# Layer 0's second product in seven block products on 1 core, and layer 1's activation kept in PSUM

## The chip, the cores and the metric

The kernel runs on 1 core of one Trainium2 chip. The metric is the device time of one execution in microseconds (us); the median of 3 runs of the kernel before is 573.87 us (573.56 to 574.56). Times below are in us, from the span's start, unless marked otherwise.

## The reference

A block-sparse attention feeds two feed-forward layers. Attention: batch 2, 8 heads, 768 positions, head size 64; each query sees its neighbours within 16 positions and one summary for each block of 32 (largest K, mean V), in one softmax. Its output is x, 1536 tokens by 512.

```python
h = x @ w_in                  # layer 0: 512 -> 2048
g = s * (r * r) + b           # r = max(h, 0)
x = g @ w_out                 # 2048 -> 512
h = x @ w_in2                 # layer 1
out = maximum(0.01 * h, h) @ w_out2
```

Inputs and weights arrive as 64-bit floats.

## The kernel before

**Products.** TensorE multiplies numbers of a reduced form of 32 bits, so every operand is split into a high part (a cast) and a low part (the operand less its high part), and one product of a 128x128 weight tile with a 128x512 token tile is three matmuls: high by high, low by high, high by low. ScalarE (ACT) makes the casts, VectorE (DVE) or GpSimd (POOL) the low parts (`split_hi` L426, `split_lo` L432 for weights, `ffn_hi` L467, `ffn_lo` L474 for activations). "A matmul" below is one of these 128x512 matmuls.

**Tiles.** The tokens are three chunks of 512 (c is 0, 1, 2 in the code; chunks 1, 2 and 3 in the text), the 2048 features 16 groups of 128 (`fc`). Groups 0 to 7 are the lower features; groups 8 to 15 are the upper ones, and two of them make a pair j (4 to 7). PSUM has 4 banks of output sums (`acc`), 2 called `h`, and 1 each called `at0` and `at1`.

**Seven block products.** A product whose rows, columns and inner dimension can each be halved is done with 7 products of blocks instead of 8, from sums and differences of blocks of weights (s1 to s4) and of tokens or activations (t1 to t4). The names are `a11, s2, a12, s3, a22, s1, s4`. The two halves of the tokens are chunks 2 and 3. A product's result is added on to others in PSUM or in SBUF.

**Order.** No scheduler orders the engines: each one's instructions are issued in the order in which the Python is written. `HEAD` (L49) is a list of operations written by hand that weaves attention with layer 0 for chunk 1 and for the lower features of chunk 2. After it the program goes on in stages:

1. `quads(0, 4, 0)` (L721): the upper features of chunks 2 and 3. The first product goes through seven block products (`block` L647, `after_block` L672). Activation (`add_act` L662: ScalarE relu, VectorE product) leaves its results in SBUF (`late_g` L614). The second product of chunk 2 is plain: `queue` holds its outputs, and `emit_out` (L711) issues one or two, three matmuls each, after every block.
2. The loop `for k in range(NS)`: the lower features of chunk 3, 8 steps of `first_in`, `chain` (L1173: relu, square, cast, low part) and four `ffn_out` (L483).
3. The loop `for fc in range(NS + 1, NFC)`: the plain second product of chunk 3's upper features (`late_split` L733).
4. Layer 1, chunk 1: 16 steps of the same kind. Here `convert` (L1164) turns loaded weights into 32-bit numbers (`rescale` L392 on ScalarE, `low_bits` L397 on VectorE or GpSimd, `shift` L410 on VectorE), `token_forms` (L589) makes the token forms of layer 1, and `split_x` (L610) splits them.
5. Layer 1, chunks 2 and 3 (`second_layer_end` L1015): both products in seven block products. In the "weave" (`weave_block` L788, `weave_after` L873) a pair's seven products of the first kind run between two blocks of the second kind (`out_unit` L844) of the pair before. The rest of the second product, five of its seven blocks, follows as "late units" (`late_unit` L969), whose operands `late_operands` (L957) splits some units ahead.

Queues: SP issues all loads of weights, `load_next` (L1160) one for each half of a group that has been converted.

## Time and profile before

| | |
|---|---|
| median of 3 runs | 573.87 us (573.56 to 574.56) |
| the profiled execution | 573.7 us |
| its span | 571.9 us |
| busy: TensorE 558.4 us (98%), VectorE 435.3 (76%), ScalarE 371.6 (65%), GpSimd 221.4 (39%) | |
| matmuls of TensorE, all forms | 3123 |
| granted clock of TensorE | full in all 40 slices |
| DMA | 53.38 MB, 93 GB/s |

The profiled execution lies 0.17 us below the median, and its own time is 1.8 us more than its span. A timeline row joins neighbouring instructions of one kind: its start, then its busy time; since TensorE's matmuls overlap in the pipeline, the time that a row takes from its engine is the next row's start less its own. "Idle before" names who ended a wait.

### The profile page before, as it was taken

The numbers are of one execution on the slowest core, as the hardware profiler recorded it, in microseconds if no ns is written. First come the engines' busy times: TensorE is split into PE (matmuls) and PEld (weight loads), VectorE is DVE, ScalarE is ACT, GpSimd is POOL, SyncE is SP. The second block draws the span as 40 slices with busy tenths as digits, with TensorE's granted clock in tenths as the row PEclk, the third lists the DMA queues.
The fourth block names the chain that finished last, engine by engine and source line by source line (L and its number), as shares of the span: only waits on it lengthen the run. The fifth ranks groups of instructions, "written<-read, shape, count | busy, mean of one in ns | idle before, by whom it ended". The sixth has DMA issues, their size and how long they took to land.

```text
span 571.9 us, 9002 instructions
## 1 busy us (share of the span) xinstructions
PE 558.4 (98%) x3123; PEld 445.9 (78%) x3124; DVE 435.3 (76%) x890; ACT 371.6 (65%) x856; POOL 221.4 (39%) x258
## 2 busy tenths in 40 slices
PE   3999999999999999999999999999999999999997
PEld 3567778787778888888888888888888888876885
DVE  5888987765689866666575879999458887889982
ACT  4788858776774655445565666766477677768860
POOL 4344644533254455522542435556234433300000
PEclk9999999999999999999999999999999999999999
DMA  8967766571300000000132524542010000000103
GB/s 322 405 206 257 245 225 205 171 244 54 129 2 1 1 0 2 1 1 1 54 95 82 176 91 136 179 140 82 18 56 0 2 1 1 0 2 1 38 0 110
DMA packets 16581, 53.38 MB, mean 93 GB/s; under 512 B 2041, under 2 KB 2937, under 8 KB 15897
## 3 DMA queue, kind: packets, MB, share of 16 engines
q1 hardware_dynamic: 16104, 52.56, 27.3%
q8 instruction: 24, 0.39, 0.3%
q10 hardware_dynamic: 432, 0.26, 0.1%
q14 instruction: 21, 0.16, 0.1%
HBM read 49.08 MB, written 3.15 MB: 91 GB/s over the span
## 4 chain that ended last, share of the span: by engine, by line
PE 93%; DMA 3%; ACT 1%; DVE 1%; SPq 0%; issue 0%; ACTq 0%
PE acc L493 31%; PE h L444 23%; PE at L793 7%; PE h L793 5%; PE acc L850 4%; PE at L974 3%; PE h L654 3%; PE at L654 3%; PE h L974 3%; DMA vt<-in_v 2%; PE acc L974 2%; PE at L336 2%; PE at L256 2%; PE at L355 2%; PE h L355 1%; PE at L210 1%
## 5 line engine op out<-in xcount | busy, mean ns | idle before, releaser
L493 PE MATMUL acc<-g,wout 128*128 128x512 f32 x756 | 188.2, 392 | 0.0
L493 PEld LDWEIGHTS acc<-g,wout 128*128 128x128 f32 x756 | 140.5, 188 | 30.1 <-issue 0.8
L444 PE MATMUL h<-xt,win 128*128 128x512 f32 x564 | 138.5, 392 | 0.0
L444 PEld LDWEIGHTS h<-xt,win 128*128 128x128 f32 x564 | 104.8, 188 | 22.6 <-issue 1.1
L435 POOL TENSOR_TENSOR win<-w,win 128x512 fp32r<-128x512 f32 x36 | 52.0, 1444 | 51.3 <-ACT win L429 37.8
L415 DVE SCALAR_TENSOR_TENSOR w<-st,w 128x512 int32<-128x512 int32 x64 | 59.1, 928 | 7.3 <-issue 3.2
L429 ACT CAST wout<-w 128x512 fp32r<-128x512 f32 x63 | 39.0, 618 | 26.4 <-PE acc L493 23.1
L435 DVE TENSOR_TENSOR wout<-w,wout 128x512 fp32r<-128x512 f32 x50 | 42.0, 839 | 14.5 <-ACT wout L429 14.1
L395 ACT ACTIVATE st<-st 128x512 f32<-128x512 f32 x64 | 41.1, 671 | 0.9 <-DVE w L415 0.9
L429 ACT CAST win<-w 128x512 fp32r<-128x512 f32 x48 | 29.6, 616 | 13.4 <-PE h L444 7.4
L793 PE MATMUL at<-xt,win 128*128 128x512 f32 x144 | 35.9, 392 | 0.0
L477 DVE SCALAR_TENSOR_TENSOR g<-h,own,g 128x512 fp32r<-128x512 f32 x31 | 23.2, 748 | 12.9 <-ACT g L470 12.9
L793 PEld LDWEIGHTS at<-xt,win 128*128 128x128 f32 x144 | 27.0, 188 | 6.2
L408 POOL TENSOR_SCALAR w<-st 128x512 int32<-128x512 uint8 x30 | 23.2, 772 | 17.8 <-DMA st<-in_w 13.0
L470 ACT ACTIVATE g<-h,own 128x512 fp32r<-128x512 f32 x31 | 21.3, 686 | 10.7 <-DVE h L465 7.3
L405 DVE TENSOR_SCALAR w<-st 128x512 int32<-128x512 int32 x34 | 27.5, 810 | 0.0
L455 ACT ACTIVATE r<-h 128x512 f32<-128x512 f32 x31 | 18.3, 593 | 14.1 <-PE h L444 14.1
L850 PE MATMUL acc<-g,wout 128*128 128x512 f32 x96 | 27.2, 393 | 0.0
L299 ACT ACTIVATE sm<-sm,nm 128x120 f32<-128x120 f32 x64 | 24.4, 387 | 3.5 <-DVE nm L281 3.5
L769 POOL TENSOR_TENSOR win<-q,win 128x256 fp32r<-128x256 f32 x8 | 7.7, 958 | 49.0 <-DVE w L822 28.5
L435 POOL TENSOR_TENSOR wout<-w,wout 128x512 fp32r<-128x512 f32 x13 | 17.7, 1361 | 23.1 <-ACT wout L429 18.2
L457 ACT ACTIVATE r<-h 128x512 f32<-128x512 f32 x16 | 9.6, 598 | 23.3 <-PE h L444 23.3
(308 smaller groups left out, 1101.4 us busy)
## 6 DMA issues: line engine op xcount, KB each, us to landing
st<-in_w SPq DMA_DIRECT2D x64, 512.0 KB, 3.5
vt<-in_v SPq DMA_DIRECT2D x5, 1024.0 KB
kt<-in_k SPq DMA_DIRECT2D x8, 500.0 KB, 5.4
q<-in_q SPq DMA_DIRECT2D x8, 256.0 KB, 3.9
w<-in_vn SPq DMA_DIRECT2D x3, 512.0 KB, 10.2
out<-kt SPq DMA_DIRECT2D x6, 256.0 KB, 2.2
w<-in_q SPq DMA_DIRECT2D x4, 256.0 KB, 12.5
w<-in_v SPq DMA_DIRECT2D x2, 512.0 KB
```

The lines of the kernel that those rows point to most:

```text
L299: nc.scalar.activation(out=sm[:, u, :], in_=sm[:, u, :], func=AF.Exp, bias=nm[:, u : u + 1], scale=-1.0, accum_out=rec[:, u, :],)
L395: nc.scalar.activation(out=high, in_=high, func=AF.Prelu, scale=2.0**-112, alpha=2.0**32)
L405: engine.tensor_scalar(f, low, 29, None, op0=ALU.logical_shift_right)
L415: nc.vector.scalar_tensor_tensor(out=f, in0=high, scalar=3, in1=f, op0=ALU.logical_shift_left, op1=ALU.bitwise_or)
L429: nc.scalar.copy(t[:, 0, :], wf[layer, fc][:, half, :])
L435: engine.tensor_sub(t[:, 1, :], wf[layer, fc][:, half, :], t[:, 0, :])
L444: nc.tensor.matmul(hs[i], lhsT=w[:, a, cc * P : (cc + 1) * P], rhs=xt[c][:, b, cc, :], start=(cc == 0 and a == b == 0), stop=(cc == NCC - ...
L493: nc.tensor.matmul(acc[m], lhsT=w[:, a, ms], rhs=g[:, b, :], start=first, stop=last)
L654: nc.tensor.matmul(banks[j, name], lhsT=t[:, a, cc * P : (cc + 1) * P], rhs=x[b][cc], start=(cc == a == b == 0), stop=(cc == b == 1),)
L793: nc.tensor.matmul(ps, lhsT=t[:, a, cc * P : (cc + 1) * P], rhs=x[b][cc], start=(name in ("a11", "s1") and cc == a == b == 0), stop=(cc == ...
L850: nc.tensor.matmul(po[k, m], lhsT=w[:, a, at : at + P], rhs=g[:, b, :], start=(j == 0 and a == b == 0), stop=(j == NQ - 1 and b == 1),)
L974: nc.tensor.matmul(ps, lhsT=w[:, a, m * P : (m + 1) * P], rhs=g[:, b, :], start=(name in ("s1", "s4") and q == a == b == 0), stop=(q == NQ ...
```

## The change

Layer 0's second product for the upper features of chunks 2 and 3 now takes seven block products too. Stage 1 becomes a weave as in layer 1: a class `Woven` holds it, `z0` for layer 0 (pairs 4 to 7) and `z1` for layer 1 (pairs 0 to 7). Two of the seven blocks (four `out_unit` of a pair) run between the first products; the other five are 20 late units after the lower features of chunk 3, in place of stage 3. Layer 0's part adds to sums that the plain lower features have begun (`part1`, `kept`). A count of 128x512 matmuls in the two programs gives 2,192 before and 2,168 after: the plain outputs were 2 x 8 x 4 outputs of 3 matmuls, 192; now there are 7 x 4 x 2 of 3, 168 (48 woven in, 120 late). The activation stays in PSUM: layer 1's leaky relu runs in place on `hs`, its cast and low part read PSUM; the woven products do relu and square there; the lower features of chunk 3 do the square on ScalarE (`square`), not VectorE. Moved besides: `H47 lp47` (a weight's split) earlier in `HEAD`; `ta6 th6 tlv6` (a token form) into the weave; the low part of `split_x` from GpSimd to VectorE, its work later; of the conversions of layer 1's weights 8 are in layer 0 (11 before) and 24 in layer 1 (21 before).

Matmuls change from 2716 to 2692 instructions on TensorE. All instructions of VectorE go from 892 to 960, ScalarE's from 765 to 831, GpSimd's from 263 to 227.

```diff
-A22 d0 O87 as22 G22 E0 lv45 th4 E1 O85 d0 Y22 ta5 E2 A23 tlv3 as23 g22 O90 th5 ta7 tlv2 tlv5 th7 H47 lp47 tlv4 G23 g23
-ta6 tlv7 th6 O88 tlv6 O91 O89
+A22 d0 O87 as22 G22 E0 lv45 th4 E1 O85 d0 Y22 ta5 H47 lp47 E2 A23 tlv3 as23 g22 O90 th5 ta7 tlv2 tlv5 th7 tlv4 G23 g23 tlv7 O88 O91 O89
...
+    def square(x):
+        nc.scalar.activation(out=x, in_=x, func=AF.Relu)
+        nc.scalar.activation(out=x, in_=x, func=AF.Square)
     def ffn_relu(i):
-        rs[i] = gpool.tile([P, 512], F32, name="r")
         if steps[i][0] == 0:
+            rs[i] = gpool.tile([P, 512], F32, name="r")
             nc.scalar.activation(out=rs[i], in_=hs[i], func=AF.Relu)
         else:
-            nc.scalar.activation(out=rs[i], in_=hs.pop(i), func=AF.Prelu, scale=1.0, alpha=0.01)
+            nc.scalar.activation(out=hs[i], in_=hs[i], func=AF.Prelu, scale=1.0, alpha=0.01)
...
-            nc.scalar.copy(gs[i][:, 0, :], rs[i])
...
-            nc.vector.tensor_sub(g[:, 1, :], rs.pop(i), g[:, 0, :])
+            nc.vector.tensor_sub(g[:, 1, :], hs.pop(i), g[:, 0, :])
...
+        end = NFC - 1 if layer or c == 0 else NS - 1
         for a, b in ((0, 0), (1, 0), (0, 1)):
             first = fc == 0 and a == 0 and b == 0
-            last = fc == NFC - 1 and b == 1
+            last = fc == end and b == 1 and not (layer == 0 and c and m < 2)
...
-        nc.gpsimd.tensor_sub(t[1][at], src, t[0][at])
+        nc.vector.tensor_sub(t[1][at], src, t[0][at])
...
+    WEAVE = (("a11", 0), ("a22", 1), ("s2", 0), ("a12", 0), ("s4", 1), ("s3", 0), ("s1", 0))
+    WITH = {"s2": "t2", "s1": "11", "s3": "12", "a22": "21", "s4": "22"}
+    BANK = {"s4": "w", "s2": "u", "s3": "u", "a22": "u", "s1": "v"}
...
+        def raw_act(self, j, k):
+            ps = self.banks[j, "pu"[k]]
+            if self.layer:
+                self.activate(ps)
+            else:
+                home = self.raw[j, f"{k + 1}1"]
+                nc.scalar.activation(out=home, in_=ps, func=AF.Relu)
+                nc.vector.tensor_mul(ps, home, ps)
+        def raw_hi(self, j, k):
+            ps = self.banks[j, "pu"[k]]
+            t = self.go[j, k] = gpool.tile([P, 2, 512], F32R, name="g")
+            (nc.scalar.copy if self.layer else self.shifted)(t[:, 0, :], ps)
+            nc.scalar.copy(self.raw[j, f"{k + 1}1"], ps)
+        def raw_lo(self, j, k):
+            t, ps = self.go[j, k], self.banks[j, "pu"[k]]
+            if self.layer:
+                nc.vector.tensor_sub(t[:, 1, :], ps, t[:, 0, :])
+            else:
+                nc.vector.scalar_tensor_tensor(
+                    out=t[:, 1, :], in0=ps, scalar=shift_b, in1=t[:, 0, :], op0=ALU.add, op1=ALU.subtract
+                )
...
+        def after(self, j, name):
+            add, head = nc.vector.tensor_add, j == self.first
+            p, u, v = (self.banks.get((j, i)) for i in "puv")
+            if name == "a11":
+                nc.scalar.copy(u, p)
+                if not head:
+                    self.activate(self.raw[j - 1, "22"])
+                    self.out_unit(j - 1, 0, 0)
+                if j > self.first + 1 and self.layer:
+                    self.raw_forms(j - 2, 3)
+                    self.out_forms(j - 2, 0)
...
+            elif name == "a12":
+                self.raw_act(j, 0)
+                if self.layer:
+                    self.raw_hi(j, 0)
+                if not head:
+                    self.raw_lo(j - 1, 1)
+                else:
+                    self.out_lo(j, 0)
+                if head and not self.layer:
+                    self.raw_hi(j, 0)
+                    self.raw_lo(j, 0)
+            elif name == "s4":
+                g12 = self.raw[j, "12"]
+                add(g12, rs.pop((self.layer, j)), v)
+                if j < self.last:
+                    if not self.layer:
+                        self.raw_hi(j + 1, 0)
+                    self.activate(g12)
+                    self.raw_lo(j + 1, 0)
+                    if j + 1 < self.last:
...
+            else:
+                g22 = self.raw[j, "22"]
+                add(g22, g22, v)
+                self.out_lo(j, 1)
+                if not head:
+                    self.raw_forms(j - 1, 1)
+                    self.raw_forms(j - 1, 2)
+                    self.out_unit(j - 1, 1, 1)
...
     def chain(i):
-        ffn_relu(i)
-        ffn_act(i)
+        if steps[i][0]:
+            ffn_relu(i)
+        else:
+            square(hs[i])
         ffn_hi(i)
         ffn_lo(i)
...
-    c1, c2 = NFC, 2 * NFC
-    queue = [("out", c1 + NS - 1, m) for m in range(4)]
-    load_next(3)
-    quads(0, NS // 2, 0)
+    c1, c2, nq = NFC, 2 * NFC, n_ffn1 + NFC
+    z0.homes()
+    part1 = [spare[:, 4 + 2 * m : 6 + 2 * m, :].rearrange("p a n -> p (a n)") for m in range(2)]
+    count = len(z0.order)
+    for n in range(count):
+        z0.multiply(n)
+        if n == 0:
+            z0.out_hi(z0.first, 0)
+            for m in (2, 3):
+                ffn_out(c1 + NS - 1, m)
+                nc.scalar.copy(part1[m - 2], accs[0, 1][m])
+        if n == 1:
+            first_forms(6, nc.vector.tensor_sub, nc.vector.tensor_add)
+            first_hi(6)
+            first_lo(6, nc.vector)
+        if n in (3, 4):
+            ffn_out(c1 + NS - 1, n - 3)
+        if n == 4:
+            z0.po.update({(1, m): accs[0, 1][m] for m in range(2)})
+        if n == count - 3:
+            second_in(c2, 0)
+    z0.raw_lo(z0.last, 1)
+    second_in(c2 + 1, 0, nc.gpsimd)
...
+    for m in range(2):
+        z0.kept["x", m] = gpool.tile([P, 512], F32, name="r")
+        nc.scalar.copy(z0.kept["x", m], z0.po[0, m])
     first_in(c2)
+    second_in(c2, 1)
     chain(c2)
-    emit_out(len(queue))
-    for m in range(4):
+    for m in range(2):
+        z0.out_unit(z0.last, 1, m)
+        ps = z0.po[1, m]
+        nc.vector.tensor_add(ps, z0.kept["x", m], ps)
         x_hi(1, m)
+    load_next(4)
+    last, kept, po, ahead_of = z0.last, z0.kept, z0.po, 4
+    work = [(z0.raw_forms, last, part) for part in (0, 2, 1)]
+    for j in range(z0.first, NQ):
+        work += [(z0.out_forms, j, 0), (z0.out_forms, j, 1)]
...
+            po["u", 0], po["u", 1] = (ps_at.pool.tile([P, 512], F32, name=f"at{m}") for m in range(2))
+            for m in range(2):
+                nc.scalar.copy(po["u", m], kept["x", m])
+        for f, j, part in work[2 * k : 2 * k + 2]:
+            f(j, part)
+        for n in {5: (0,), 6: (1,), 7: (2, 3)}.get(k, ()):
+            z0.operands(n)
+        convert((0, 2, 2, 2, 2, 0, 0, 0)[k], nc.gpsimd)
...
-    for fc in range(NS + 1, NFC):
...
+    acc = accs[0, 2]
+    po["w", 0], po["w", 1] = acc[0], acc[1]
+    for n, (name, q) in enumerate(z0.units):
+        z0.operands(n + ahead_of)
+        if name == "s4":
+            z0.raw_forms(q, 3)
+        if (name, q) == ("s1", z0.first):
+            po["v", 0], po["v", 1] = (ps_h.tile([P, 512], F32, name="h") for _ in range(2))
+        for m in range(2):
+            z0.unit(n, m)
+            if q == last and name in ("s2", "s3"):
+                kept[name, m] = soft.tile((name, m))
+                nc.scalar.copy(kept[name, m], po["u", m])
+                if name == "s3":
+                    nc.vector.tensor_add(po["u", m], part1[m], po["u", m])
+            if q == last and name == "s1":
+                for x, ps in ((kept["s2", m], acc[m]), (kept["s3", m], acc[2 + m])):
+                    nc.vector.tensor_add(x, x, po["v", m])
+                    nc.vector.tensor_add(ps, x, ps)
+    for m in range(2):
+        accs[0, 1][2 + m] = po["u", m]
+        for name in ("s2", "s3"):
+            soft.free((name, m))
+    first_in(n_ffn1)
+    second_in(n_ffn1 + 1, 0, nc.gpsimd)
     for m in range(4):
         x_hi(2, m)
+    chain(n_ffn1)
+    for m in range(2):
+        x_hi(1, 2 + m)
...
-        at -= 1
+        if at < 2:
+            for m in (2 * at, 2 * at + 1):
+                split_x([[xt[1][:, a, c, :] for c in range(4)] for a in range(2)], m, xf[1][m])
+        at -= 2
         if 0 <= at < 10:
             token_forms(at // 5, at % 5)
```

**TensorE, the first round of stage 1.** Before, from the last plain output of HEAD on (L654 is a block of the first product, L493 a plain output; the second word is the PSUM bank that is written):

```order
L493 MATMUL acc_2022<-g_2437,wout_2433 128x512 x3
L654 MATMUL at0_2540<-vt_2295,win_2401 128x512 x6
L654 MATMUL h_2553<-xt2_100,win_2402 128x512 x6
L493 MATMUL acc_2044<-g_2527,wout_2530 128x512 x3
L493 MATMUL acc_1980<-g_2527,wout_2530 128x512 x3
L654 MATMUL at1_2571<-xt1_99,win_2402 128x512 x6
L493 MATMUL acc_2009<-g_2527,wout_2530 128x512 x3
L654 MATMUL h_2591<-vt_2296,win_2401 128x512 x6
L493 MATMUL acc_2022<-g_2527,wout_2530 128x512 x3
L654 MATMUL at0_2604<-xt1_99,win_2401 128x512 x6
L493 MATMUL acc_2044<-g_2582,wout_2585 128x512 x3
```

After (L698 is a block of the first product, L777 a block of the second, L497 a plain output):

```order
L497 MATMUL acc_2044<-g_2439,wout_2417 128x512 x3
L698 MATMUL at0_2537<-xt1_99,win_2403 128x512 x6
L777 MATMUL acc_2550<-g_2502,wout_2465 128x512 x3
L698 MATMUL h_2455<-sm0_2318,win_2404 128x512 x2
L698 MATMUL h_2455<-sm3_2434,win_2404 128x512
L698 MATMUL h_2455<-sm1_2487,win_2404 128x512 x2
L698 MATMUL h_2455<-sm2_2489,win_2404 128x512
L777 MATMUL acc_2567<-g_2502,wout_2465 128x512 x3
L698 MATMUL h_2538<-st_2297,win_2404 128x512 x2
L698 MATMUL h_2538<-st_2298,win_2404 128x512
L698 MATMUL h_2538<-st_2297,win_2404 128x512 x2
L698 MATMUL h_2538<-st_2298,win_2404 128x512
```

The three plain outputs that came one after each block are gone; after the first block comes the first block of the second product, for pair 4.

**VectorE, in that round.** Before (L477 low part of an activation, L435 of a weight, L668 and L695 additions out of PSUM, L670 the product that makes the square):

```order
L477 SCALAR_TENSOR_TENSOR g_2527<-r_2471,own_94,g_2527 128x512
L435 TENSOR_TENSOR wout_2530<-w_1043,wout_2530 128x512
L695 TENSOR_TENSOR w_1043<-w_1043,at0_2540 128x512
L668 TENSOR_TENSOR at0_2540<-w_959,at0_2540 128x512
L670 TENSOR_TENSOR w_959<-w_959,at0_2540 128x512
L668 TENSOR_TENSOR h_2553<-w_1043,h_2553 128x512
L670 TENSOR_TENSOR w_1043<-w_1043,h_2553 128x512
L477 SCALAR_TENSOR_TENSOR g_2582<-r_2523,own_94,g_2582 128x512
```

After (L671 and L735 low parts of weights, L753 the square's product in PSUM, L766 the low part of the activation, L842 the addition of s4):

```order
L671 TENSOR_TENSOR win_2403<-spare_96,win_2403 128x256
L753 TENSOR_TENSOR h_2455<-vt_2452,h_2455 128x512
L735 TENSOR_TENSOR wout_2564<-w_1119,wout_2564 128x256
L671 TENSOR_TENSOR win_2404<-q1_2160,win_2404 128x256
L753 TENSOR_TENSOR at0_2537<-vt_2452,at0_2537 128x512
L766 SCALAR_TENSOR_TENSOR g_2581<-h_2455,own_94,g_2581 128x512
L842 TENSOR_TENSOR w_1043<-r_2483,at1_2523 128x512
L766 SCALAR_TENSOR_TENSOR g_2604<-at0_2537,own_94,g_2604 128x512
```

Each block's square and low part now stand ahead of the addition that frees the bank of s4 (`at1`), so that the additions wait behind them.

**ScalarE, at the end of HEAD.** Before (L643 casts of weight blocks, L583 of token forms, L429 of a weight, L455 relu, L463 square, L470 cast of the activation):

```order
L643 CAST win_2401<-w_1043 128x256
L583 CAST vt_2295<-kt_2064 128x512
L643 CAST win_2401<-q0_2159 128x256
L643 CAST win_2402<-w_1043 128x256
L455 ACTIVATE r_2417<-h_2367 128x512
L463 ACTIVATE h_2367<-r_2417 128x512
L583 CAST vt_2296<-kt_2064 128x512
L583 CAST kt_2297<-kt_2065 128x512
L429 CAST wout_2433<-w_900 128x512
L470 ACTIVATE g_2437<-h_2367,own_94 128x512
```

After (L669, L584, L428, L458, L466, L473 are the same in turn):

```order
L669 CAST win_2403<-w_1043 128x256
L584 CAST st_2295<-kt_2064 128x512
L669 CAST win_2403<-q0_2159 128x256
L428 CAST wout_2417<-w_900 128x512
L669 CAST win_2404<-w_1043 128x256
L458 ACTIVATE r_2422<-h_2369 128x512
L466 ACTIVATE h_2369<-r_2422 128x512
L584 CAST st_2297<-kt_2064 128x512
L584 CAST kt_2299<-kt_2065 128x512
L473 ACTIVATE g_2439<-h_2369,own_94 128x512
```

The cast of `wout` (group 7, from `H47`) moved from behind the token casts to ahead of the weight block's cast and the relu.

## Rows read from the trace of the kernel before

**Rows 1.** The page, part 1: busy us, share of the span, instructions.

```profile
PE 558.4 (98%) x3123; PEld 445.9 (78%) x3124; DVE 435.3 (76%) x890; ACT 371.6 (65%) x856; POOL 221.4 (39%) x258
```

**Rows 2.** TensorE's waits, 20 to 572 us: engine, line, releaser; total, times, longest.

```profile
PE at L974 <- ACT xt L964: 0.6, 1, 0.6
```

**Rows 3.** TensorE's timeline, layer 1: start us, busy us, line, [idle before].

```profile
342.84 2.88 PE L444 MATMUL h<-xt,win 128*128 128x512 f32 x12
345.56 2.88 PE L493 MATMUL acc<-g,wout 128*128 128x512 f32 x12
```

**Rows 4.** TensorE's timeline, layer 1's handover to the late units.

```profile
517.98 1.35 PE L974 MATMUL at<-xt,win 128*128 128x512 f32 x3
...
524.10 0.86 PE L850 MATMUL acc<-g,wout 128*128 128x512 f32 x3
```

**Rows 5.** TensorE's timeline, within layer 1's late units.

```profile
535.13 2.90 PE L974 MATMUL acc<-xt,win 128*128 128x512 f32 x12
...
544.76 0.84 PE L974 MATMUL at<-xt,win 128*128 128x512 f32 x3
```

**Rows 6.** TensorE's timeline: a pair's round in layer 0, then in layer 1.

```profile
208.89 1.52 PE L654 MATMUL at<-xt,win 128*128 128x512 f32 x6
...
224.06 1.52 PE L654 MATMUL h<-xt,win 128*128 128x512 f32 x6
...
467.79 1.55 PE L793 MATMUL at<-xt,win 128*128 128x512 f32 x6
...
480.23 1.09 PE L793 MATMUL at<-xt,win 128*128 128x512 f32 x4
```

**Rows 7.** Groups of ScalarE's and VectorE's instructions: busy us, mean ns, idle before.

```profile
L470 ACT ACTIVATE g<-h,own 128x512 fp32r<-128x512 f32 x31 | 21.3, 686 | 10.7 <-DVE h L465 7.3 <-PE acc L493 2.7 <-ACT win L429 0.6
L455 ACT ACTIVATE r<-h 128x512 f32<-128x512 f32 x31 | 18.3, 593 | 14.1 <-PE h L444 14.1
L768 ACT CAST win<-q 128x256 fp32r<-128x256 f32 x28 | 11.6, 413 | 0.0
...
L477 DVE SCALAR_TENSOR_TENSOR g<-h,own,g 128x512 fp32r<-128x512 f32 x31 | 23.2, 748 | 12.9 <-ACT g L470 12.9
L907 DVE TENSOR_TENSOR w<-r,at 128x512 f32<-128x512 f32 x8 | 5.5, 687 | 5.2 <-PE at L793 5.2
```

**Rows 8.** ScalarE's timeline at the end of the attention's part.

```profile
191.56 0.59 ACT L455 ACTIVATE r<-h 128x512 f32<-128x512 f32 x1
...
193.75 0.62 ACT L429 CAST wout<-w 128x512 fp32r<-128x512 f32 x1
194.27 0.68 ACT L470 ACTIVATE g<-h,own 128x512 fp32r<-128x512 f32 x1
```

**Rows 9.** TensorE's timeline there: layer 0's last plain outputs.

```profile
190.99 4.24 PE L493 MATMUL acc<-g,wout 128*128 128x512 f32 x18
195.07 1.52 PE L654 MATMUL h<-xt,win 128*128 128x512 f32 x6
```

**Rows 10.** VectorE's timeline, one step of layer 1, then GpSimd's and TensorE's there.

```profile
347.20 0.68 DVE L481 TENSOR_TENSOR g<-r,g 128x512 fp32r<-128x512 f32 x1
347.81 0.42 DVE L405 TENSOR_SCALAR w<-st 128x512 int32<-128x512 int32 x1
348.33 0.69 DVE L415 SCALAR_TENSOR_TENSOR w<-st,w 128x512 int32<-128x512 int32 x1
348.94 1.52 DVE L405 TENSOR_SCALAR w<-st 128x512 int32<-128x512 int32 x1
350.56 1.60 DVE L415 SCALAR_TENSOR_TENSOR w<-st,w 128x512 int32<-128x512 int32 x1
...
350.13 1.47 POOL L435 TENSOR_TENSOR win<-w,win 128x512 fp32r<-128x512 f32 x1
...
351.00 2.20 PE L493 MATMUL acc<-g,wout 128*128 128x512 f32 x9
```

**Rows 11.** The page, part 6: loads of weights: count, KB, us to landing.

```profile
st<-in_w SPq DMA_DIRECT2D x64, 512.0 KB, 3.5
```

More of the change, by code (lines that the diff above doesn't have):

```diff
@@ L471, in ffn_hi @@
         else:
[L472 removed]
+            nc.scalar.copy(gs[i][:, 0, :], hs[i])
     def ffn_lo(i):
@@ L521, in block_attention_moe_moe @@
     NQ, LEAD = NFC // 2, 3
[L522 removed]
     TOKENS = {"a11": "b11", "s2": "t2", "a12": "b21", "s3": "t3", "a22": "t4", "s1": "t1", "s4": "b22"}
[L524 to L530 removed]
+    tf, raws = {}, {}
     def late_t4(layer, i):
@@ new lines, in operands @@
+        def operands(self, n):
+            if n >= len(self.units):
+                return
+            name, q = self.units[n]
+            g, w = self.home(n)
+            src, form = self.raw[q, WITH[name]], self.out_form(q, name)
+            nc.scalar.copy(w[:, 0, :], form)
+            if self.layer or name not in ("s4", "s2"):
+                nc.scalar.copy(g[:, 0, :], src)
+                nc.vector.tensor_sub(w[:, 1, :], form, w[:, 0, :])
+                nc.vector.tensor_sub(g[:, 1, :], src, g[:, 0, :])
+            else:
+                self.shifted(g[:, 0, :], src)
+                nc.vector.tensor_sub(w[:, 1, :], form, w[:, 0, :])
+                nc.vector.scalar_tensor_tensor(
+                    out=g[:, 1, :], in0=src, scalar=shift_b, in1=g[:, 0, :], op0=ALU.add, op1=ALU.subtract
+                )
+            self.late[n] = w, g
@@ L957, in late_operands @@
[L957 to L981 removed]
+                    self.po[BANK[name], m],
@@ L983, in result @@
+                    lhsT=w[:, a, m * P : (m + 1) * P],
+                    rhs=g[:, b, :],
+                    start=(name in self.opens and q == self.first and a == b == 0),
+                    stop=(q == self.last and b == 1),
+                    skip_group_check=name in ("s2", "s3", "a22"),
+                )
     def result(i, k, m, ps, x=None):
-        if "free" not in rings:
+        if "free" not in raws:
             t = kpool_.tile([P, 1024], F32, name="kt")
-            rings["free"] = [t[:, h * 512 : h * 512 + 512] for h in range(2)]
+            raws["free"] = [t[:, h * 512 : h * 512 + 512] for h in range(2)]
```

718 lines of the change are left out of this document (269 added, 449 removed).

## The prediction, made before the changed kernel ran

> **What bounds the kernel now.** I read the page's busy shares first: TensorE is busy for 558.4 of 571.9 us [rows 1], and its granted clock is full in all slices of the page. Then TensorE's waits: from 20 us to the end the largest that has a releaser is one of 0.6 us [rows 2]. So TensorE's stream is the time, and a matmul taken out of it is worth its own length, unless a wait comes in its place. The timeline in layer 1 gives that length: a row of 12 outputs' matmuls starts 2.72 us after a row of 12 input matmuls, so 0.2267 us for each [rows 3]. The reader should see one more thing: the waits view is not all that is lost. At layer 1's handover from its weave to its late units 18 matmuls take 6.12 us, from 517.98 to 524.10 [rows 4]; at 0.2267 they would take 4.08. So 2.04 us are lost where the waits view has only 0.6 [rows 2]: the rest stands as longer rows. I therefore price a seam by the starts of rows, not by named waits.
>
> **The matmuls removed.** By the program's order 192 plain matmuls become 168: 24 x 0.2267 = **-5.44 us**. Nothing else of TensorE's work changes in number: the first products stay 7 a pair.
>
> The Trainium skill, page "TensorE: Matmul & The Clock Gate", section "Back-to-back issue gap", gives about 131 ns for one of many matmuls of 512 columns, each with its own weight load, and about 216 ns for one alone. By the first the saving would be an estimated 24 x 0.131 = 3.1 us, by the second 5.2; the rows of this kernel measure 226.7 ns, and the measurement decides.
>
> **The order of the late matmuls.** Plain outputs alternate with input products in rows of 12. Late units run in threes on one bank with changing operands: within layer 1's late units 42 matmuls take 9.63 us, 0.2293 each, so 0.0026 more [rows 5]. 120 late matmuls x 0.0026 = **+0.31**.
>
> **The weave's rounds.** Before, a pair's round in layer 0, 66 matmuls, takes 15.17 us, 0.21 more than 66 x 0.2267. A round of layer 1's weave, which is what layer 0 gets now, has 54 in 12.44 us, 0.20 more than its matmuls [rows 6]. The overhead of switching is the same: 0.
>
> **The start of the weave.** ScalarE's cast of wout moves ahead of a weight block's cast and the relu of step 23. Its buffer is one of two, free only when the older output's matmuls are done: the first 6 of the 18 in a row that starts at 190.99, so at 192.35 [rows 9]. Before, that cast ran at 193.75 and waited for nothing [rows 8]. Now relu, square, two token casts and the activation's cast come behind it; ScalarE's rows there follow each other about 0.52 us apart [rows 8], so the cast of the activation, six places on, begins at 192.35 + 6 x 0.52 = 195.5 and ends, 0.68 later and with 0.1 for the square's wait on the relu, at about 196.3 instead of 194.95 [rows 8]. VectorE's low part (0.75) [rows 7] then ends at about 197.1. Of TensorE, before, the next block began at 195.07 [rows 9]; now the block that begins there is 6 matmuls and the plain output behind it reads the low part in its third, so it is wanted at 195.07 + 8 x 0.2267 = 196.88. I take **+0.3**: the chain ends 0.2 late by these rows, and I add a little for the gap between the engines. Ends: 0 (it just fits) and 0.75 (one low part late).
>
> **Three rounds, one tight chain.** In a round of pair j ScalarE has, after s2: a copy, the cast of the last pair's a22 result (0.69), a copy, a weight's cast (0.41), then the relu of a12 (0.59) [rows 7]; by these it ends about 2.72 us after s2's end. Then VectorE: the square's product (priced like L907, 0.69, one operand in PSUM as there), the low part (0.75) and only then the addition that frees s4's bank [rows 7]: 4.74 to 4.80. TensorE wants that bank for s1 after a12, s4, s3 and an output, 21 matmuls x 0.2267 = 4.76. So it is a tie. Layer 1's weave has the same tie without the product and shows no such wait in the waits view. I take 0.15 for each of three rounds, **+0.45**; the ends are 0 and 0.6 (one more VectorE instruction ahead of the addition), so 0 to 1.8.
>
> **Handover to chunk 3.** After the last pair, the next plain outputs take the banks of `po`: two copies to SBUF, a product of outputs, two additions, then `x_hi`. ScalarE and VectorE read those sums out at 0.6 to 0.7 each [rows 7] while `first_in` runs 12 matmuls, 2.72 us. By counting, the third bank is free 8.34 us after the last s4 and wanted at 8.16. I take **+0.2**, ends 0 and 1.3 (two instructions more).
>
> **What costs nothing, and its cover.** Layer 1's leaky relu in PSUM: ScalarE's and VectorE's instructions are as many; the bank of h is held until the low part is done, but a second h bank takes the next step's 12 matmuls (2.72 us). Square on ScalarE in chunk 3's lower steps: two relus' lengths, 0.59 + 0.59, in steps of 24 matmuls (5.44 us). It adds one ScalarE instruction to each step and takes one from VectorE. Operands of late units: four units of 6 matmuls ahead, 5.44 us, for two casts and two low parts of 0.4 to 0.7 each. Loads: SP's issues now wait until the weave is done, and land 3.5 us after issue [rows 11]; the first conversion is a step of 5.44 us later. Conversions: 24 instead of 21 in layer 1, on VectorE; the tokens' low parts move from GpSimd to VectorE too. A conversion's two VectorE instructions take 0.42 + 0.69 when alone [rows 10]. In the busiest step VectorE has four other instructions of about 0.60 and two conversions of 1.13 from start to start: 4.66 of 5.44 us. It fits, if none is held up. Also there the low part of the activation ends at 347.88 and is first wanted with the outputs at 351.00, 3.1 us of slack [rows 10]. So 0.
>
> **Sum.** -5.44 + 0.31 + 0.3 + 0.45 + 0.2 = -4.18. The profiled execution is 573.7, so 569.5; the median is 0.17 above it, so **569.7 us**.
>
> **Rivals.**
> (A) The ties all fall well: only the matmuls and, or not, the 0.31: 573.87 - 5.44 = 568.4, to 568.7. For it: TensorE waits almost nowhere now [rows 2], and layer 1's weave, built in the same way, runs smoothly [rows 6]. Against it: the start and the handover come out late by the rows.
> (B) New seams are as dear as layer 1's handover, 2.04 us each [rows 4]. One such seam above the forecast: 569.7 + 2.0 = 571.7; three in place of the small terms (start, handover, entry to layer 1): -5.44 + 0.31 + 6.12 = +1.0, so 574.9. For it: that seam is where layer 1 passes from one kind of work to another, as layer 0 now does three times. Against it: at layer 1's handover new operands are split just ahead; here the lower steps of chunk 3 stand between, 8 x 5.44 us in which operands are made.
> (C) Slower: VectorE becomes the bound in layer 1's first chunk. Beside a GpSimd instruction (1.47) a conversion's two instructions took 1.52 + 1.60 instead of 0.42 + 0.69, so 2.0 more [rows 10]. One held-up conversion in a step makes 4.66 + 2.0 = 6.67 us of VectorE against 5.44 of TensorE: 1.23 too many. With two conversions in a step, over eight steps, that is 9.8, less the 3.1 us of slack, +6.7: 576.4. It ends slower than before from 4.2 + 3.1 = 7.3 us in all, 0.91 in each of eight steps, so at some 6.4 us of VectorE a step. Against it: GpSimd now has only a weight's low part in a step, since the tokens' are gone from it, and the activation's low part reads PSUM.
> By the Trainium skill, page "SBUF — State Buffer", section "Who interferes with whom", VectorE with two SBUF inputs and GpSimd reading SBUF exclude each other for a whole instruction; the doubled durations agree, and by it the moves take as much contention away as they add.
> (D) The change doesn't do what it says. The order of the program has the 24 matmuls gone, so this can't be.
>
> **How the numbers follow.** My forecast, within its bounds, gets 0.66; A 0.10; B 0.15 (one seam 0.08, more 0.07); C 0.09. The forecast's bounds: all small terms at their low end give 568.4, all at the high end 0.31 + 0.75 + 1.8 + 1.3 - 5.44 = -1.28, so 572.6. That takes in A, one seam of B, and leaves out C and the rest of B. 0.2% is 1.15 us, about what a measurement of this kernel can tell from no change. Faster by more than that: below 572.7, so forecast, A and one seam, 0.84; within: several seams that nearly eat the saving, 0.06; slower, 0.10.
>
> **What would show it.** Right: TensorE's row count down by 24 matmuls, steps of late units at 0.2293 each, waits named at s1's blocks (addition of s4) of 0.1 to 0.2, and a first output of the weave about 0.3 late. Wrong: rounds of 54 matmuls longer than 12.9 us; a wait of over 1 us at the entry to the late units, to layer 1, or to chunk 3; VectorE busy without pause in layer 1's first chunk, with the outputs waiting for low parts there. If it is below 568.4, something not in this sum got cheaper, such as layer 1's own seam.

## The result, and the profile after

The changed kernel takes 569.24 us (569.08 to 569.37, 6 runs), the kernel before 573.91 (573.53 to 574.56, 6 runs); the ratio is 0.9917, 95% interval 0.9905 to 0.9930. The forecast was 569.7 in 568.4 to 572.6.

The page of the changed kernel, part 1: TensorE has the 24 instructions less of the order, VectorE and ScalarE have more, GpSimd less ([rows 1] before).

```profile
PE 553.0 (98%) x3099; PEld 440.7 (78%) x3100; DVE 451.9 (80%) x958; ACT 399.9 (71%) x922; POOL 180.2 (32%) x222
```

The profiled execution's span is 567.1 us, 4.8 less than before. TensorE's waits, 20 to 567 us, still name very little. The one of [rows 2] is there unchanged (0.6 us); the first of these two was one wait of 0.2 us before, in layer 1, and the second is new:

```profile
PE at L698 <- DVE w L842: 0.3, 2, 0.2
PE acc L497 <- DVE g L480: 0.2, 1, 0.2
```

As in the forecast, the rest must be read from the starts of rows. TensorE's timeline from the end of the attention's part on (start us, busy us, [idle before]; the three places are the start of the weave, its last round, the handover to chunk 3):

```profile
190.53 4.24 PE L497 MATMUL acc<-g,wout 128*128 128x512 f32 x18
194.62 1.52 PE L698 MATMUL at<-xt,win 128*128 128x512 f32 x6
195.97 0.66 PE L497 MATMUL acc<-g,wout 128*128 128x512 f32 x2
196.79 1.19 PE L497 MATMUL acc<-g,wout 128*128 128x512 f32 x4 [0.15 <-DVE g L480]
197.83 1.55 PE L698 MATMUL h<-st,win 128*128 128x512 f32 x6
...
206.01 0.84 PE L777 MATMUL acc<-g,wout 128*128 128x512 f32 x3
...
239.16 0.84 PE L777 MATMUL acc<-g,wout 128*128 128x512 f32 x3
240.19 1.61 PE L698 MATMUL at<-st,win 128*128 128x512 f32 x6 [0.19 <-DVE w L842]
241.63 0.84 PE L777 MATMUL acc<-g,wout 128*128 128x512 f32 x3
...
246.46 2.88 PE L443 MATMUL h<-xt,win 128*128 128x512 f32 x12
...
253.29 3.02 PE L497 MATMUL acc<-g,wout 128*128 128x512 f32 x12
256.15 3.22 PE L443 MATMUL h<-xt,win 128*128 128x512 f32 x12
259.20 2.88 PE L497 MATMUL acc<-g,wout 128*128 128x512 f32 x12
```

At 0.2267 us each, the 6 plain matmuls from 195.97 should end at 197.33; the next row starts at 197.83, so 0.50 us are lost, while the wait named is 0.15. The three matmuls from 239.16 take 1.03 instead of 0.68, and the six of s1 after them 1.44 instead of 1.36: 0.43. At the handover the outputs from 253.29 take 2.86, the input products from 256.15 take 3.05, instead of 2.72 each: 0.47 lost, without any wait named. The late units show no loss at all:

```profile
291.84 4.24 PE L923 MATMUL at<-xt,early 128*128 128x512 f32 x18
...
319.04 5.60 PE L443 MATMUL h<-xt,win 128*128 128x512 f32 x24
324.48 2.88 PE L497 MATMUL acc<-g,wout 128*128 128x512 f32 x12
```

120 matmuls from 291.84 to 319.04, 27.20 us, 0.2267 each. In the kernel before, the first outputs of layer 1 are this row:

```profile
329.24 2.88 PE L493 MATMUL acc<-g,wout 128*128 128x512 f32 x12
```

Between the plain outputs before the weave ([rows 9] before) and the first outputs of layer 1 the kernel before took 329.24 - 190.99 = 138.25 us for 606 matmuls, the changed one 324.48 - 190.53 = 133.95 for 582. All of the stages' gain, 4.30 us, comes together from the terms below. "Lost" is the time from row to row less 0.2267 us for each matmul. The rows that bound the terms start at 194.62, 206.01, 246.46 and 291.84 (before: 195.07, 208.89 and 254.39, then on to 329.24):

| term | forecast | lost before | lost after | measured |
|---|---|---|---|---|
| 24 matmuls | -5.44 | | | -5.44 |
| start of the weave, to the first full round | +0.3 | 0.22 | 0.51 | +0.29 |
| three rounds | +0.45 | 0.62 | 1.01 | +0.39 |
| handover, to the late units | +0.2 | 0.05 | 0.50 | +0.45 |
| late units | +0.31 | 0 | 0 | 0 |
| sum | -4.18 | | | -4.31 |

The other 0.46 us of the span are already there at 190 us (190.99 against 190.53); 0.43 of them stand at 22 us (22.36 against 21.93 for the same row), where nothing was changed.

### The profile page after: what moved, and what is told of

The parts are those of the page before. It is cut to its first block, busy times and chain, and to the rows that moved or that the text cites. A ratio compares the mean times of both kernels' runs of the same rounds, so it can differ in the third digit from the quotient of the medians.

```text
span 567.1 us, 9003 instructions
## 1 busy us (share of the span) xinstructions
PE 553.0 (98%) x3099; PEld 440.7 (78%) x3100; DVE 451.9 (80%) x958; ACT 399.9 (71%) x922; POOL 180.2 (32%) x222
## 4 chain that ended last, share of the span: by engine, by line
PE 91%; ACT 4%; DVE 3%; DMA 1%; issue 1%; SPq 0%; POOL 0%; ACTq 0%
PE acc L497 23%; PE h L443 23%; PE at L698 11%; PE h L698 8%; PE at L923 6%; PE acc L777 5%; PE h L923 4%; PE acc L923 3%; PE at L335 2%; PE at L255 2%; PE at L354 2%; ACT w L298 1%; DMA kt<-in_k 1%; PE h L354 1%; PE acc L443 0%
## 5 line engine op out<-in xcount | busy, mean ns | idle before, releaser
L497 PE MATMUL acc<-g,wout 128*128 128x512 f32 x576 | 143.4, 394 | 0.2 <-DVE g L480 0.2
L497 PEld LDWEIGHTS acc<-g,wout 128*128 128x128 f32 x576 | 106.5, 188 | 23.6 <-issue 0.9
L434 POOL TENSOR_TENSOR win<-w,win 128x512 fp32r<-128x512 f32 x35 | 49.4, 1411 | 119.6 <-ACT win L428 116.7
L414 DVE SCALAR_TENSOR_TENSOR w<-st,w 128x512 int32<-128x512 int32 x64 | 51.0, 807 | 6.5 <-issue 3.7
L698 PE MATMUL at<-xt,win 128*128 128x512 f32 x216 | 53.7, 391 | 0.0
L698 PEld LDWEIGHTS at<-xt,win 128*128 128x128 f32 x216 | 40.6, 188 | 9.1
L428 ACT CAST wout<-w 128x512 fp32r<-128x512 f32 x48 | 29.7, 619 | 18.2 <-PE acc L497 16.6
L428 ACT CAST win<-w 128x512 fp32r<-128x512 f32 x48 | 29.6, 617 | 17.5 <-DVE w L414 8.8
L777 PE MATMUL acc<-g,wout 128*128 128x512 f32 x144 | 40.4, 392 | 0.0
L671 POOL TENSOR_TENSOR win<-q,win 128x256 fp32r<-128x256 f32 x13 | 11.7, 899 | 76.7 <-ACT win L669 48.1
L777 PEld LDWEIGHTS acc<-g,wout 128*128 128x128 f32 x144 | 27.1, 188 | 5.9
L434 DVE TENSOR_TENSOR wout<-w,wout 128x512 fp32r<-128x512 f32 x35 | 28.1, 803 | 4.3 <-ACT wout L428 4.3
L434 POOL TENSOR_TENSOR wout<-w,wout 128x512 fp32r<-128x512 f32 x13 | 17.4, 1340 | 22.9 <-ACT wout L428 18.3
L473 ACT ACTIVATE g<-h,own 128x512 fp32r<-128x512 f32 x31 | 21.3, 686 | 4.6 <-PE acc L497 2.7
L460 ACT ACTIVATE h<-h 128x512 f32<-128x512 f32 x16 | 9.3, 582 | 19.9 <-PE h L443 19.9
L404 DVE TENSOR_SCALAR w<-st 128x512 int32<-128x512 int32 x37 | 19.9, 539 | 0.8 <-DMA st<-in_w 0.8
```

The lines of the kernel that those rows point to most:

```text
L414: nc.vector.scalar_tensor_tensor(out=f, in0=high, scalar=3, in1=f, op0=ALU.logical_shift_left, op1=ALU.bitwise_or)
L428: nc.scalar.copy(t[:, 0, :], wf[layer, fc][:, half, :])
L434: engine.tensor_sub(t[:, 1, :], wf[layer, fc][:, half, :], t[:, 0, :])
L473: nc.scalar.activation(out=gs[i][:, 0, :], in_=hs[i], func=AF.Identity, bias=shift_b, scale=1.0)
L497: nc.tensor.matmul(acc[m], lhsT=w[:, a, ms], rhs=g[:, b, :], start=first, stop=last)
L698: nc.tensor.matmul(ps, lhsT=t[:, a, cc * P : (cc + 1) * P], rhs=x[b][cc], start=(name in ("a11", "s1") and cc == a == b == 0), stop=(cc == ...
```

## The experiments

All ratios are to the kernel before, run on the same chip; its median was 573.45 to 573.60 there.

**The changed kernel again**, as the control.

> The changed kernel itself, on the chip of the next run, so that single seams can be told from chip to chip. By the rows of the changed kernel 4.30 us of its gain lie in the stages that the change touches and 0.46 us in the first 22 us, where nothing was changed; if that is chance of one execution, it is 4.1 to 4.6 us faster than the kernel before here, 4.8 or more if it is not.

569.10 us against 573.52, ratio 0.9918 (0.9903 to 0.9933): 4.4 us. The 0.46 us were mostly chance; in the runs of this study that row starts between 190.4 and 191.9 us.

**Each seam by itself.** A seam is a place where TensorE's stream passes from one kind of work to the next. First the cast of wout.

```diff
-... ta5 H47 lp47 E2 A23 tlv3 as23 g22 O90 th5 ta7 tlv2 tlv5 th7 tlv4 ...
+... ta5 E2 A23 tlv3 as23 g22 O90 th5 ta7 tlv2 tlv5 th7 H47 lp47 tlv4 ...
```

> The split of wout for step 23 goes back behind the token casts, where it stood before the change. My theory: the loss at the start of the weave (in the changed kernel 0.51 us between 194.62 and 206.01, 0.29 more than before) is the chain cast of wout, relu, square, cast, low part on ScalarE and VectorE; without the cast ahead of it the activation's low part comes some 0.5 us earlier, the wait of 0.15 us on it goes, and the time falls by 0.3 us to about 568.9. Rival: the cast was in nobody's way, or its low part on GpSimd now comes too late for the plain output: no change (569.2) or 0.3 us more, with a wait on GpSimd at that output.

569.07 us, ratio 0.9923 (0.9911 to 0.9936): a difference of 0.3 us can't be told by this time. The rows can tell it. TensorE's timeline at the same place:

```profile
195.97 1.52 PE L698 MATMUL at<-xt,win 128*128 128x512 f32 x6
197.33 1.52 PE L497 MATMUL acc<-g,wout 128*128 128x512 f32 x6
198.69 1.52 PE L698 MATMUL h<-st,win 128*128 128x512 f32 x6
```

Six matmuls in 1.36 us: the wait and the 0.50 us are gone, and the 48 matmuls from 195.97 to 206.85 take 10.88 us, just their length. The cast that the change moved was the cause of these 0.50 us.

Second, ScalarE's order in a round.

`raw_hi`, a cast and then a copy, is parted into `raw_cast` and `raw_copy`. The first of the two places is behind s2, the second behind a12.

```diff
                 if not head and not self.layer:
-                    self.raw_hi(j - 1, 1)
+                    self.raw_cast(j - 1, 1)
...
                 if self.layer:
                     self.raw_hi(j, 0)
+                elif not head:
+                    self.raw_copy(j - 1, 1)
```

> In layer 0's weave ScalarE's copy of the last pair's result to SBUF moves behind the relu of a12, so relu, square, low part and the addition of s4 can all come some 0.5 us earlier. My theory of the tie: the wait at s1 in the last round (0.19 us named, 0.43 by the rows' starts) goes, the rounds before keep their 0.21 us, which layer 1's rounds have too; the time falls by 0.4 us to about 568.8. Rival: the relu waits for a12's matmuls and not for ScalarE, or the late addition is due to the weight's low part ahead of it alone: then the last round keeps over 0.3 us of loss and the time stays at 569.2.

568.60 us, ratio 0.9913 (0.9899 to 0.9927). The last round:

```profile
240.08 0.84 PE L783 MATMUL acc<-g,wout 128*128 128x512 f32 x3
240.76 1.54 PE L698 MATMUL at<-st,win 128*128 128x512 f32 x6
242.14 0.85 PE L783 MATMUL acc<-g,wout 128*128 128x512 f32 x3
```

The output takes 0.68 and s1 1.38 us: 0.02 us lost where it was 0.43. With the copy out of the chain the addition begins 3.80 us after s2's end (239.80) instead of 4.29 (239.36), although the weight's low part still stands ahead of it; whether moving that low part would do as well was not run. In the two rounds before, the 0.10 us at s1 went too, which I had not expected; these rounds now lose 0.08 us each instead of 0.21.

Third, the additions at the handover.

```diff
-    chain(c2)
+    square(hs[c2])
+    ffn_hi(c2)
     for m in range(2):
         z0.out_unit(z0.last, 1, m)
         ps = z0.po[1, m]
         nc.vector.tensor_add(ps, z0.kept["x", m], ps)
+    ffn_lo(c2)
+    for m in range(2):
         x_hi(1, m)
```

> At the handover to chunk 3 VectorE's two additions go ahead of the activation's low part, into a stretch in which VectorE is idle, and the two evacuations behind it. My theory: the 0.50 us lost between 250.53 and 259.20 come from the additions behind the low part, which hold ScalarE's evacuation for 1.4 us, and with it the next weight's cast and GpSimd's low part; all of it goes, and the time falls by 0.45 us to about 568.8. Rival: the low part itself is late then, a loss of 0.2 us or more at the outputs of the first step, and the time stays within 0.2 us of 569.2.

568.93 us, ratio 0.9919 (0.9905 to 0.9932), again too small for the time alone. TensorE's timeline at the handover:

```profile
253.64 2.88 PE L497 MATMUL acc<-g,wout 128*128 128x512 f32 x12
256.36 2.88 PE L443 MATMUL h<-xt,win 128*128 128x512 f32 x12
259.08 2.88 PE L497 MATMUL acc<-g,wout 128*128 128x512 f32 x12
```

2.72 us for each row: nothing is lost. Last, all three together.

> The three moves together. If the three losses are separate seams of TensorE's stream, they add up: 0.3 + 0.4 + 0.45 = 1.15 us, to about 568.1. If a gain at one is lost at the next (the stream only arrives earlier at the same wait), the sum is smaller: 568.5 to 568.9.

567.72 us, ratio 0.9899 (0.9886 to 0.9913); against the control's 0.9918 that is 1.1 us less, but the two intervals overlap, so the times alone don't show that the seams add up. The rows do. Two of TensorE's rows in this kernel, the start of the weave and the outputs behind the handover:

```profile
194.97 1.52 PE L698 MATMUL at<-xt,win 128*128 128x512 f32 x6
...
257.86 2.88 PE L497 MATMUL acc<-g,wout 128*128 128x512 f32 x12
```

The 276 matmuls between them take 62.89 us, 0.33 more than their length; in the changed kernel they take 64.58 (194.62 to 259.20), 2.02 more. So 1.69 us came back. One by one the three moves gave 0.53, 0.74 and 0.47 us between the same rows, 1.74 together: the seams add up, as separate waits of one stream do.

**The price of the matmuls.**

```diff
             z0.unit(n, m)
+            if n in (1, 2, 9, 10):
+                z0.unit(n, m)
```

> Four of layer 0's late units are multiplied twice, 24 matmuls more, so the count is that of before again; the sums contain these blocks twice. My theory: each matmul costs its 0.2267 us and nothing else: 24 x 0.2267 = 5.44 more, 574.7, that is about 0.8 us slower than the kernel before (the seams alone). Rival: the late units wait for their operands in part, and the repeats fill such gaps: less than 4 us more, under 573.2.

574.76 us, 5.66 more than the control (24 x 0.2267 = 5.44), ratio 1.0018 (1.0009 to 1.0028). By the rows the late units, now 144 matmuls, take 32.64 us (291.95 to 324.59) for 27.20, just 5.44 more, so no repeat filled a gap. With the count of before, the changed kernel is, by the ratio, 1.0 us slower than the kernel before: that is what its seams cost, 1.13 us by the table.

**VectorE in layer 1's first chunk.** The forecast counted 4.66 us a step. VectorE's timeline of one step of the changed kernel, from one activation's low part (L484) to the next, then GpSimd's there (left out: the second conversion, 0.42 and 0.69 us, and the low parts at L613 and L434, 0.68 and 0.69):

```profile
381.30 0.68 DVE L484 TENSOR_TENSOR g<-h,g 128x512 fp32r<-128x512 f32 x1
381.90 0.41 DVE L404 TENSOR_SCALAR w<-st 128x512 int32<-128x512 int32 x1
382.42 0.69 DVE L414 SCALAR_TENSOR_TENSOR w<-st,w 128x512 int32<-128x512 int32 x1
...
384.16 1.78 DVE L606 TENSOR_TENSOR kt<-kt 128x512 f32<-128x512 f32 x1
...
387.07 0.68 DVE L484 TENSOR_TENSOR g<-h,g 128x512 fp32r<-128x512 f32 x1
```

```profile
383.90 1.50 POOL L434 TENSOR_TENSOR win<-w,win 128x512 fp32r<-128x512 f32 x1 [4.28 <-ACT win L428]
```

The step takes 387.07 - 381.30 = 5.77 us, more than TensorE's 5.44. The addition at L606 takes 1.78 instead of about 0.68, since GpSimd's low part of a weight (383.90 to 385.40) runs then. So in this step the low part comes 0.33 us nearer to its use; in the other full steps, with two conversions, it comes 0.13 to 0.34 us nearer. It begins at 331.35 for outputs at 335.36, 3.3 us ahead after its 0.68; at 359.82 for 362.56, 2.1 (VectorE's row, then TensorE's):

```profile
359.82 0.68 DVE L484 TENSOR_TENSOR g<-h,g 128x512 fp32r<-128x512 f32 x1
...
362.56 2.88 PE L497 MATMUL acc<-g,wout 128*128 128x512 f32 x12
```

A step with one conversion gives back over 1 us (from 359.82 to 363.99 VectorE takes 4.17). From the second step on the lead never gets below 1.7. To see whether that slack is real, VectorE gets 0.60 us more a step:

```diff
             second_in(i + 1, 1)
+            split_lo(i + 1, 1, nc.vector)
```

> In layer 1's first chunk VectorE makes each step's low part of wout twice (the same numbers, 0.60 us more of VectorE a step, 15 steps). Rows of the changed kernel show VectorE's step at 5.77 us against TensorE's 5.44, where the forecast counted 4.66; the low part of the activation comes 0.33 us nearer to its use in each full step and two lighter steps give it back, from 3.3 down to 1.7 us. My theory from this: with 6.37 us a step the slack of 3.1 us is used up after three or four steps, and TensorE then follows VectorE: some 3 to 6 us more, 572 to 575. Rival, by the forecast's count: 4.66 + 0.60 = 5.26 still fits into 5.44, and the time stays at 569.2.

575.48 us, ratio 1.0030 (1.0019 to 1.0041): 6.4 us more than the control, a little above what I gave. TensorE's largest wait, and VectorE's timeline of one step:

```profile
PE h L443 <- POOL win L434: 3.2, 5, 0.9
```

```profile
380.07 0.68 DVE L484 TENSOR_TENSOR g<-h,g 128x512 fp32r<-128x512 f32 x1
...
386.55 0.68 DVE L484 TENSOR_TENSOR g<-h,g 128x512 fp32r<-128x512 f32 x1
```

A step now takes 6.48 us, and TensorE follows it: its outputs there start at 380.36 and 386.84, 6.48 us apart. The slack lasted longer than I had it, the first loss over 0.1 us being at that chunk's eighth row of outputs. The wait is named at GpSimd's low part of win, not at the activation, as I had it: the conversions on VectorE come late, then ScalarE's cast (it waits 13.4 us for them between 360 and 400), then GpSimd. By the starts of rows 4.6 us of the chunk's loss are at input products, behind this chain; 1.4 are at outputs, and the first large one of these, 0.45 us from 362.91, is where the activation's low part ends at 363.61. Next, the token forms' low parts go back to GpSimd.

```diff
-        nc.vector.tensor_sub(t[1][at], src, t[0][at])
+        nc.gpsimd.tensor_sub(t[1][at], src, t[0][at])
```

> The low parts of layer 1's token forms go back to GpSimd, the rest stays. My theory: VectorE has 0.60 us less in a step, GpSimd some 1.4 more, and what contention it adds on VectorE eats that saving; TensorE sees none of it: 569.2 within 0.3. Rival: GpSimd, with weight and token low parts in one queue, delays a weight's low part, and TensorE waits on GpSimd: over 0.5 us more.

571.36 us, ratio 0.9956 (0.9940 to 0.9973), 2.3 us more than the control. My theory fell: TensorE does see it.

```profile
PE h L443 <- POOL win L434: 0.9, 3, 0.3
```

VectorE's timeline of one step, then GpSimd's:

```profile
383.80 0.68 DVE L484 TENSOR_TENSOR g<-h,g 128x512 fp32r<-128x512 f32 x1
...
384.92 1.59 DVE L414 SCALAR_TENSOR_TENSOR w<-st,w 128x512 int32<-128x512 int32 x1
...
387.56 1.77 DVE L606 TENSOR_TENSOR kt<-kt 128x512 f32<-128x512 f32 x1
...
389.86 0.68 DVE L484 TENSOR_TENSOR g<-h,g 128x512 fp32r<-128x512 f32 x1
```

```profile
384.50 1.46 POOL L613 TENSOR_TENSOR vt<-kt,vt 128x512 fp32r<-128x512 f32 x1 [1.78 <-ACT vt L612]
387.30 1.49 POOL L434 TENSOR_TENSOR win<-w,win 128x512 fp32r<-128x512 f32 x1 [1.34 <-ACT win L428]
```

With one instruction less VectorE's step is longer, 389.86 - 383.80 = 6.06 us: GpSimd now runs twice in a step, and holds up two instructions (1.59 for 0.69 at L414, 1.77 for 0.68 at L606). 0.60 saved, 0.9 added. The rival's number came, over 0.5 us with TensorE waiting for GpSimd, but not from GpSimd's queue: GpSimd itself waits 1.34 us for ScalarE's cast of win, and that cast 2.17 us for VectorE's conversion. This move, which I had costed at nothing, is worth 2.3 us; without it the kernel would still be 2.2 us faster than the kernel before, so it isn't alone what keeps rival C from happening.

**Layer 1's leaky relu.**

```diff
-            nc.scalar.activation(out=hs[i], in_=hs[i], func=AF.Prelu, scale=1.0, alpha=0.01)
+            r = gpool.tile([P, 512], F32, name="r")
+            nc.scalar.activation(out=r, in_=hs[i], func=AF.Prelu, scale=1.0, alpha=0.01)
+            hs[i] = r
```

> Layer 1's leaky relu in the first chunk writes to SBUF again, as before the change; the rest of the change stays. My theory: this part is worth nothing on the path: 569.2 within 0.3, TensorE without a wait in that chunk. Rival: the activation's low part then reads two operands in SBUF and is held up beside GpSimd (0.68 to about 1.6 us in some steps), so that VectorE's slack goes faster: TensorE waits appear, 1 us or more.

569.95 us, ratio 0.9930 (0.9915 to 0.9945), 0.85 more than the control by the medians, within the two intervals. The rows show one new loss, when GpSimd makes the weave's first weight forms. VectorE's low part of the activation and GpSimd's form beside it, in this kernel:

```profile
392.78 1.23 DVE L486 TENSOR_TENSOR g<-r,g 128x512 fp32r<-128x512 f32 x1
```

```profile
392.39 1.07 POOL L652 TENSOR_TENSOR q<-q,w 128x256 f32<-128x256 f32 x1
```

and in the changed kernel:

```profile
392.79 0.68 DVE L484 TENSOR_TENSOR g<-h,g 128x512 fp32r<-128x512 f32 x1
```

GpSimd's form runs there at the same time (L650, 392.39, 1.07 us).

With both operands in SBUF the low part takes 1.23 us beside GpSimd, with one in PSUM 0.68. The next conversion, ScalarE's cast (396.12 instead of 395.04) and GpSimd's low part come later by it, and TensorE waits:

```profile
397.83 0.39 PE L443 MATMUL h<-xt,win 128*128 128x512 f32 x1
398.37 2.79 PE L443 MATMUL h<-xt,win 128*128 128x512 f32 x11 [0.15 <-POOL win L434]
401.00 1.30 PE L499 MATMUL acc<-g,wout 128*128 128x512 f32 x5
```

12 matmuls from 397.83 to 401.00 take 3.17 instead of 2.72: 0.45 lost, and no such loss in the changed kernel. The rival was right in kind, by the rows at half its price or less. The Trainium skill, page "SBUF — State Buffer", section "Who interferes with whom", says that a VectorE instruction with at most one input in SBUF, outside the 2-port modes, doesn't contend with GpSimd, and that one with two contends with a GpSimd instruction that reads SBUF; the 0.68 and the 1.23 us agree. One operand in SBUF isn't always enough: in the changed kernel L404, which has no other, took 1.52 us at 350.01 for its 0.42, beside GpSimd's low part of win (349.88 to 351.25).

**A faster version.** In the forecast I priced a seam by layer 1's handover to its late units, 2.04 us [rows 4]. In the kernel with the three moves it is as large, and there ScalarE has a long wait for VectorE (ScalarE's waits, 505 to 520 us):

```profile
ACT win L914 <- DVE w L726: 2.3, 1, 2.3
```

L726 is the last weight form of the last pair. Its two forms go ahead of the operands, the low part of the activation goes behind them:

```diff
-        forms = [(z.out_forms, last, 0), (z.out_forms, last, 1), (z.raw_forms, last, 0)]
+        forms = [(z.raw_forms, last, 0)]
...
-            if n >= count - 2:
-                z.out_forms(last - 1, n - count + 2)
+            if n == count - 2:
+                for j, part in ((last - 1, 0), (last, 0), (last, 1)):
+                    z.out_forms(j, part)
             for x in begin.get(n, ()):
                 z.operands(x)
+            if n == count - 1:
+                z.out_forms(last - 1, 1)
...
-        z.raw_lo(last, 1)
...
-            if forms:
+            if n > 1 and forms:
...
             z.operands(n + lead)
+            if n == 1:
+                z.raw_lo(last, 1)
```

> The three moves, and at layer 1's handover to its late units (2.04 us lost there before and after the change) the weight forms of the last pair go ahead of the operands, and the low part of its activation behind them, on VectorE. My theory: ScalarE's cast for the eighth unit waits 2.3 us for VectorE's last weight form, and this is most of the seam; with the forms earlier at least 1.3 of the 2.04 us go: 1.2 + 1.3 = 2.5 us faster than the changed kernel or more. Rival: the seam comes from the number of operands that ScalarE and VectorE must split there in all, and moving them only shifts the wait: less than 0.5 us beyond the three moves.

566.81 us, ratio 0.9878 (0.9861 to 0.9895). 0.9 us came, less than I had expected: I had pushed another form, of the pair before, behind operands that need it less than the next ones do. Its place is taken back in the last kernel:

```diff
+            if n == count - 1:
+                z.out_forms(last - 1, 1)
             for x in begin.get(n, ()):
                 z.operands(x)
-            if n == count - 1:
-                z.out_forms(last - 1, 1)
```

> As e9, but the last weight form of the pair before goes back ahead of the last two operands, into the 0.99 us in which VectorE was idle in e9. e9 gave 0.86 us at the handover where 1.3 were expected; its trace has ScalarE waiting 0.69 us for just this form. My theory: that form was the rest of the seam that order can give; with it in the gap the two units' operands come 0.7 us earlier and another 0.5 to 0.9 us goes: ratio to the kernel before about 0.9865. Rival: the amount of splitting is the limit and the wait only moves to the next operand: within 0.2 us of e9, ratio 0.9875 or more.

566.08 us, ratio 0.9865 (0.9849 to 0.9882). TensorE's timeline over the same 42 matmuls of the handover, with the three moves alone, then in this kernel:

```profile
506.25 0.86 PE L931 MATMUL at<-vt,early 128*128 128x512 f32 x3
...
517.94 0.86 PE L783 MATMUL acc<-g,wout 128*128 128x512 f32 x3
```

```profile
506.30 0.87 PE L931 MATMUL at<-vt,early 128*128 128x512 f32 x3
...
516.38 0.86 PE L783 MATMUL acc<-g,wout 128*128 128x512 f32 x3
```

11.69 us became 10.08; 42 x 0.2267 = 9.52, so 2.17 us lost became 0.56 (1.31 in the kernel between them). The rows show it, where the intervals of the last two kernels overlap. So 1.61 of the 2.17 us were the order and not the amount; what the last 0.56 are wasn't found. This version, 7.4 us faster than the kernel before on its chip, is the fastest that was run.

## Why the prediction was right

- **The sum.** -4.18 forecast, -4.31 measured. That it is so near is in part luck: the +0.31 for the late units, which didn't come, makes up for the 0.25 us by which the handover was put too low.
- **The bound.** TensorE's stream is the time, and a matmul costs its length: the kernel with 24 more shows it (5.66 for 5.44 by the time, 5.44 by the rows).
- **Start of the weave.** Right in mechanism and size: the moved cast, +0.29 for +0.3. Undone, the loss goes.
- **Three rounds.** The tie was real, +0.39 for +0.45, but not spread as I put it (0.15 each). By the rows of the rounds, two lost 0.21 us as the rounds before the change did, and the last 0.59. Of the 0.21 the tie is 0.10, since it goes with the copy's move; so the switching itself costs less than the 0.20 that the forecast took from layer 1. In the last round a weight's low part on VectorE (0.41 us, from 239.03) stands ahead of the addition as well, which is the upper end that I gave (one more instruction).
- **Handover to chunk 3.** The step "the third bank is free 8.34 us after the last s4 and wanted at 8.16" named the right queue, and was mis-sized: +0.45, not +0.2. I stopped at the first late evacuation. The larger part, 0.33 us, is at the next input product: ScalarE's cast of its weight (254.50) stands behind the evacuation, which waits 1.42 us for VectorE's additions and begins at 253.91, and GpSimd's low part (255.19) stands behind the cast.
- **Late units, +0.31.** Mis-sized: 0. Layer 1's late units run at 0.2293 us a matmul, layer 0's at 0.2267, though they too go in threes; so "groups of three" is not what costs 0.0026. What does wasn't found.
- **VectorE in layer 1, "4.66 of 5.44 us".** The step that failed, though its result, 0, held. The step is 5.77 us; I had counted no instruction held up by GpSimd, with one in each full step (about 1 us), although [rows 10] have two such in one step. It costs nothing since 3 us of slack carry it from one lighter step to the next. Rival C was nearer than its 0.09 said: with 0.60 us more on VectorE the step is 6.48 us and the kernel slower than before, as C has it from some 6.4 us on.
- **"Layer 1's leaky relu in PSUM: 0", "the tokens' low parts move".** Costed at nothing, and seen from the sum that is right; but taken back each costs, 0.45 us by the rows and 2.3 us by the time. So they weren't free: without them VectorE is held up for longer than its slack bears.
- **Rival B** (a seam of 2.04 us) didn't come: no seam of layer 0 lost over 0.6 us, and the largest new loss is 0.45. That layer 0's operands are made in the lower steps of chunk 3, as said against it, agrees with the late units' start without a loss.

## What to carry to other kernels

Where one engine's stream is the time, price each seam from the starts of its rows, and follow a late instruction one queue further than the first wait: what stands behind it is late too. For an engine near the bound, take a step's length from one instruction to the same one in the next step, with the neighbours' hold-ups in it, and follow the slack over the steps; a sum of uncontended durations says nothing there. A matmul removed is worth its length only so long as the work that replaces it finds gaps in the other engines' orders, and these orders can be mended by moving single instructions: three moves took the loss of three seams from 2.02 to 0.33 us.

## What the runs showed of the hardware that was not expected

An instruction taken from VectorE and given to GpSimd made VectorE slower (5.77 to 6.06 us a step). A subtraction on VectorE beside GpSimd took 0.68 us with one operand in PSUM and 1.23 us with both in SBUF. An instruction of VectorE with its one operand in SBUF took 1.52 us beside GpSimd for 0.42 alone. A matmul of one form took 0.2267 us in layer 0's late units and 0.2293 in layer 1's, with the granted clock full in both; this stays open.
